# Loading the stacked queries of an attention half with one transfer instead of three

## The chip, the cores and the metric

The kernel runs on one core of a Trainium2 chip. The core has a matrix engine (TensorE, PE in the profile; its weight loads are listed apart as PEld), a vector engine (VectorE, DVE), a scalar engine (ScalarE, ACT), a general engine (GpSimd, POOL) and SyncE (SP), which in this kernel issues every transfer and does nothing else but pass on a few semaphores. Data lies in DRAM, in the on-chip memory SBUF (128 partitions) and in the eight accumulator banks of PSUM. Sixteen DMA engines move data between DRAM and SBUF.

The metric is the device time of one execution in microseconds, as the median of several runs. The kernel before takes 1583.15 us (three runs, 1582.33 to 1583.36).

## The reference

One input `x` of 2048 rows and 512 columns goes through an attention block with one shared key and value head and through a gated feed-forward block; a gate per row mixes the two.

```python
q = (x @ wq)            # 32 heads of 16 columns
k, v = x @ wk, x @ wv   # one head of 16 columns, shared by all 32
p = softmax(q @ k.T * 16 ** -0.5)
a = (p @ v, heads side by side) @ wo
b = (sigmoid(x @ w_gate) * (x @ w_up)) @ w_down      # 512 -> 1792 -> 512
g = sigmoid((x * gate_w).sum(-1))
out = g * a + (1 - g) * b
```

## The kernel before, in words

**Two numbers for one.** Products of projections and scores are made from a high part in the rounded type `fp32r` and a low part, the rest: `a*b` is taken as `hi*hi + hi*lo + lo*hi`. For the scores, whose inner dimension is a head's 16 columns, the three products are stacked into one inner dimension: three groups of 16 rows on each side, 48 rows in all. On the query side the stack is high part, high part again, low part. Rows 62 and 63 of each half of 64 partitions carry the high and low part of the negated row maximum.

**Units.** The 2048 queries are cut into 4 blocks of 512 (`TB`), and the 32 heads into 8 groups of 4 heads (`NG`). One block of one group is a unit; there are 32 (`NU`). A unit's four heads sit in two halves of the partitions (`par`, rows 0 to 47 and 64 to 111) with two heads beside each other in the free dimension (`pr`). A unit's stacked queries are the tile `qs`, 128 by 2 by 512; three such tiles take turns (`qs_t[u % 3]`).

**What happens to a unit's queries.** `query` multiplies a block with the query weights; `query_out` (lines 948 and 949) copies the result as the high part on ScalarE and takes the low part on VectorE. `store_q` (line 955) writes the two parts to a DRAM tile `qd`, which has room for two units. `load_q` (lines 969 and 971) fetches from it the rows of one unit into `qs`: for each half three transfers of 16 rows, the high part twice and the low part once, and from the fourth unit on a transfer that puts zeros into rows 62 and 63 (`qs` and `zeros`). Every row of such a transfer is 4 KB that lie together in DRAM. Then come the matmuls of `maximum` (line 1136), whose results VectorE reduces to row maxima (line 1138); the maxima go through GpSimd, VectorE and DRAM (`md`) and back into rows 62 and 63 (`place_max`, line 1002), and after that `scores` (line 1145) and the exponential on ScalarE (line 1147). Both kinds of matmul work on halves of the matrix engine: one on rows 0 to 63, one on rows 64 to 127, in turn.

**The order.** A planner in the kernel (class `State`) replays a string of codes, one code for a step of the matrix engine, and lays down the order of all instructions of all engines before anything is built; it carries due times of its own, and nothing is decided on the chip. Each engine runs its instructions in this order, and so does SP with its transfers. When a step of `load_q` comes is decided by the planner: as soon as the maxima of the unit before last are through (`load_next`), about one unit ahead of use except for the first two units, which are loaded right after the first two stores. The planner counts six issues and 384 KB for a unit; these numbers are not edited.

**SP's semaphores.** The transfers take eight semaphores in turn (`DMAHW0` to `DMAHW7`). A transfer that would take a semaphore waits until the transfer eight places before it has landed, and while it waits everything behind it on SP waits too. SP also relays between the two halves of a feed-forward bank: line 1114 is an empty instruction on SP that a matmul of the other half (line 1110) waits for.

**Two other loads have a form that matters here.** `vd<-od` (line 1039) and `bc<-rd` (line 1053) fetch 64 rows of 2 KB as four blocks of 16 rows: in DRAM the outermost count is 4, in SBUF it is 64 rows. All the other large transfers have the same number of rows, 16 or 128, outermost on both sides.

Of the kernel before, what the change touches and what calls it, by code (L numbers as in the profile page):

```python
# [9 lines left out]
F32 = mybir.dt.float32  # L10
# [7 lines left out]
S, D, H, DH, F = 2048, 512, 32, 16, 1792  # L18
P = 128
TB = 512  # L20
# [705 lines left out]
def tile_kernel(ctx, tc, x_in, wq, wkv, wo, wg, wu, wd, consts_in, out):  # L726
    nc = tc.nc

    def pool(name, bufs=1, **kw):
        return ctx.enter_context(tc.tile_pool(name=name, bufs=bufs, **kw))  # L730
# [5 lines left out]
    dp = pool("dp", space=DRAM)  # L736
# [137 lines left out]
    zeros = dp.tile([2, 2 * TB], F32, name="zeros")  # L874
# [11 lines left out]
    for o in (0, 64):  # L886
        nc.vector.tensor_copy(stack_of[:, :, o:o + 48].rearrange("p kc (i d) -> p kc i d", d=DH),
                              some[:, :, :DH].unsqueeze(2).to_broadcast([P, KC, 3, DH]))
        n = 8 if o else 9
# [51 lines left out]
    QD = {}  # L941
# [8 lines left out]

    def store_q(b, t):

        qd = dp.tile([2, 2, 2, DH, 2, TB], F32, name=f"qd{b}_{t}")
        for i, half in enumerate(QD[b, t]):
            nc.sync.dma_start(qd[i].rearrange("g par d pr t -> (g par d pr) t"), f32(half))
        QD[b, t] = qd

# [5 lines left out]
    def load_q(u):  # L963
        b, g = divmod(u, NG)
        qd, qs = QD[b, g // 2], f32(qs_t[u % 3]).rearrange("p pr t -> p (pr t)")
        for par in range(2):
            for n, i in enumerate((0, 0, 1)):
                r = 64 * par + n * DH
                nc.sync.dma_start(qs[r:r + DH], qd[i, g % 2, par].rearrange("d pr t -> d (pr t)"))
            if u > 2:  # L970
                nc.sync.dma_start(qs[64 * par + 62:64 * par + 64], zeros)
        MX[u] = ap.tile([P, 2, 2, NT, 4], F32, tag="mx", name=f"mx{u}", bufs=2)

    def max_finish(u):
# [165 lines left out]
    def scores(h, n, i):  # L1140
# [10 lines left out]
        "load_x": first_x, "x_first": first_hi, "xf": first_lo, "wq_first": wq_hi, "wq": wq_lo, "keys": on_bank(keys),  # L1151
        "query": on_bank(query), "turn": on_bank(turn), "keys_out": on_bank(keys_out), "query_out": on_bank(query_out),
        "turned": on_bank(turned), "store_q": store_q, "load_q": load_q, "add_sums": add_sums,
        "load": load_item, "w_hi": w_hi, "w": w_split, "x_hi": x_hi, "x": x_lo,
        "f": fill, "gate": gate, "gated": gated, "h": h_split, "part": part_of, "add": add_part, "out": send_out,
# [31 lines left out]
    for i in range(2):  # L1187
        for j in range(4):
            for t in (2 * i, 2 * i + 1):
                r, m = HALF[t % 2], slice(32 * j, 32 * j + 32)  # L1190
                nc.tensor.matmul(ps[t][m, :], o[i][r, m], WS["last"][r], start=True, stop=True)  # L1191
    BL = [BA.pop((NB - 1, t)) for t in range(NT)]
    for t in (1, 0, 2, 3):
        ba, g = BL[t], gsig[:, n0 + t:n0 + t + 1]
# [57 lines left out]
```

## Time and profile before

| | |
|---|---|
| time, median of three runs | 1583.15 us |
| time of the profiled execution | 1581.56 us |
| its span, first to last instruction | 1579.8 us |
| PE busy | 1570.6 us, 99% of the span |
| DVE busy | 1335.6 us, 85% |
| ACT busy | 1223.0 us, 77% |
| POOL busy | 785.7 us, 50% |
| DMA engines, mean busy share | about 21% |
| granted TensorE clock | 1.0 through the whole span |

The profile is one execution. Its span is 1.8 us shorter than the time of that execution and 3.4 us shorter than the median of the other runs. Times in it are microseconds from the first instruction unless marked ns. Rows of a timeline give start, duration, engine, line, operation and tiles (`out<-in`), then a count where like instructions are merged (`x12`, the duration then is that from the first start to the last end), and in brackets the idle time ahead of it and what ended that. SPq is SP's queue; a row of it is the issue of a transfer, not the transfer. Rows for a line give the shortest, median and longest duration in ns and the first and last start. PEldq is the queue of the matrix engine: an `EVENT_SEMAPHORE` there is a wait that stands in the program ahead of a matmul, because that matmul waits for more semaphores than one instruction can name.

### The profile page before, as it was taken

Reading aid. Unit: us, or ns where it says so; the run is one execution under the profiler, and the core shown is the slowest. Engines: PE = TensorE matmul, PEld = TensorE weight load, DVE = VectorE, ACT = ScalarE, POOL = GpSimd, SP = SyncE. Lnnn points to the kernel's source line nnn. Section 1 sums busy time; section 2 is a strip of 40 time slices with the busy share of each in tenths; the row PEclk is TensorE's granted clock in tenths of the full one; section 3 lists DMA queues with packets and bytes.
Section 4 is the critical chain, followed back from the end, with each engine's and each line's share of the span. In section 5 each row is a group of like instructions: output and inputs, shape, how many; then the busy total and the mean of one; then the engine's idle time right before and its main releaser. Section 6 shows DMA issues by size and latency. Waiting matters only on the chain.

```text
span 1579.8 us, 33611 instructions
## 1 busy us (share of the span) xinstructions
PE 1570.6 (99%) x12910; PEld 1018.7 (64%) x12910; DVE 1335.6 (85%) x2280; ACT 1223.0 (77%) x2415; POOL 785.7 (50%) x713
## 2 busy tenths in 40 slices
PE   9999999999999999999999999999999999999998
PEld 7776766666666665756665666666666667676663
DVE  7998998988798888889889878897978899898852
ACT  4276778878788778868788877877878888787897
POOL 4226463745574164367466236265657426537351
PEclk9999999999999999999999999999999999999999
DMA  7413120212122121122121212022212212111011
GB/s 254 154 55 91 45 62 30 66 53 89 42 80 61 48 80 52 33 73 73 47 82 53 76 36 85 16 66 67 75 42 89 66 34 79 53 36 56 16 56 48
DMA packets 63077, 103.44 MB, mean 65 GB/s; under 512 B 24530, under 2 KB 24786, under 8 KB 62916
## 3 DMA queue, kind: packets, MB, share of 16 engines
q1 hardware_dynamic: 62916, 101.29, 20.5%
q8 instruction: 102, 1.67, 0.4%
q14 instruction: 59, 0.48, 0.1%
HBM read 79.51 MB, written 21.75 MB: 64 GB/s over the span
## 4 chain that ended last, share of the span: by engine, by line
PE 98%; DVE 1%; DMA 0%; POOL 0%; issue 0%; ACT 0%; DVEq 0%; SPq 0%; ACTq 0%
PE bank L1110 32%; PE bank L1009 29%; PE bank L1136 17%; PE bank L1145 16%; PE bank L854 3%; DVE mx L1138 1%; PE bank L1191 0%; DMA wkv_raw<-wkv 0%; POOL wkv_s L757 0%; PE bank L926 0%; DVE q L949 0%; DVE wkv_stack L890 0%; DVE ba L1200 0%; DVEq L1248 0%; ACT ou_last L1173 0%
## 5 line engine op out<-in xcount | busy, mean ns | idle before, releaser
L1138 DVE TENSOR_REDUCE mx<-bank 128x1 f32<-128x512 f32 x2048 | 1249.7, 680 | 172.9 <-PE bank L1136 85.9
L1147 ACT ACTIVATE p<-bank 128x512 f32<-128x512 f32 x2048 | 1037.2, 661 | 4.5 <-PE bank L1145 1.4
L1145 PE MATMUL bank<-qs,ks 64*128 64x512 f32 x2048 | 721.6, 401 | 0.0
L1136 PE MATMUL bank<-ks,qs 64*128 64x512 f32 x2048 | 680.7, 407 | 0.0
L1009 PE MATMUL bank<-p,v_aug 128*32 128x512 f32 x4096 | 477.5, 597 | 0.0
L1136 PEld LDWEIGHTS bank<-ks,qs 64*128 64x128 f32 x2048 | 337.5, 184 | 133.2 <-issue 49.7
L1145 PEld LDWEIGHTS bank<-qs,ks 64*128 64x128 f32 x2048 | 358.7, 184 | 89.5 <-ACT p L1147 20.1
L1016 ACT COPY ou<-bank 128x512 f32<-128x512 f32 x194 | 117.0, 603 | 281.1 <-PE bank L1009 196.0
L1023 POOL TENSOR_TENSOR ou<-ou,ou 128x512 f32<-128x512 f32 x163 | 210.0, 1288 | 210.9 <-ACT ou L1016 207.8
L1110 PE MATMUL bank<-wd,hl 64*128 64x512 f32 x1344 | 278.3, 391 | 0.1
L1110 PE MATMUL bank<-x,wu 64*128 64x512 f32 x1344 | 278.0, 391 | 0.1
L1009 PEld LDWEIGHTS bank<-p,v_aug 128*32 128x32 f32 x4096 | 114.7, 109 | 253.5 <-issue 208.5
L1110 PE MATMUL bank<-x,wg 64*128 64x512 f32 x1344 | 275.2, 391 | 0.0
L1110 PEld LDWEIGHTS bank<-wd,hl 64*128 64x128 f32 x1344 | 204.0, 184 | 19.7 <-issue 4.2
L1110 PEld LDWEIGHTS bank<-x,wu 64*128 64x128 f32 x1344 | 203.5, 185 | 14.8 <-issue 1.7
L1110 PEld LDWEIGHTS bank<-x,wg 64*128 64x128 f32 x1344 | 201.8, 185 | 16.1 <-issue 2.0
L1089 POOL TENSOR_TENSOR ba<-ba,pa_d 128x512 f32<-128x512 f32 x31 | 39.6, 1284 | 102.8 <-ACT pa_d L1086 102.8
L830 POOL CAST wg<-rg 128x1024 fp32r<-128x1024 f32 x27 | 28.0, 1038 | 123.5 <-PE bank L1110 66.2
L757 POOL TENSOR_TENSOR wd<-rd,wd 128x512 fp32r<-128x512 f32 x56 | 72.3, 1291 | 4.5
L757 POOL TENSOR_TENSOR hl<-h,hl 128x512 fp32r<-128x512 f32 x56 | 71.9, 1284 | 4.5
L1110 PE MATMUL bank<-wa,o 64*128 64x512 f32 x360 | 71.4, 393 | 0.0
L830 POOL CAST wu<-ru 128x1024 fp32r<-128x1024 f32 x27 | 28.0, 1038 | 82.1 <-PE bank L1110 65.0
(82 smaller groups left out, 745.1 us busy)
## 6 DMA issues: line engine op xcount, KB each, us to landing
rg<-wg SPq DMA_DIRECT2D x28, 512.0 KB
ru<-wu SPq DMA_DIRECT2D x28, 512.0 KB
rd<-wd SPq DMA_DIRECT2D x28, 512.0 KB
qs<-qd SPq DMA_DIRECT2D x192, 64.0 KB
qd<-q SPq DMA_DIRECT2D x32, 256.0 KB
od<-ou SPq DMA_DIRECT2D x31, 256.0 KB
xf<-x_in SPq DMA_DIRECT2D x16, 256.0 KB
vd<-od SPq DMA_DIRECT2D x32, 128.0 KB
```

The costliest lines, as they stand in the source:

```text
L757: lo.tensor_tensor(hl[:, 1, :], raw, f32(hl[:, 0, :]), op=ALU.subtract)
L830: nc.gpsimd.tensor_copy(WS[item][:, 0, :], raw)
L854: nc.tensor.matmul(ps, w[:, p, part(kc)], X[b, kc][:, q, :], start=i == 0, stop=i == 3 * KC - 1)
L1009: nc.tensor.matmul(ps[32 * j:32 * j + 32, :], v_aug[:, c, :], PT.pop((u, c, j)), start=start, stop=stop)
L1016: nc.scalar.copy(to, ps)
L1023: nc.gpsimd.tensor_tensor(SUMS[u], SUMS[u], PARTS_OF[u].pop(0), op=ALU.add)
L1089: nc.gpsimd.tensor_tensor(BA[b, t], BA[b, t], PA[b, t].pop(0), op=ALU.add)
L1110: ins = nc.tensor.matmul(banks[i], l, r, start=start, stop=stop)
L1136: nc.tensor.matmul(banks[i], qs_t[u % 3][r, pr, part(qt)], ks[r, kb * 512:(kb + 1) * 512], start=True, stop=True)
L1138: nc.vector.tensor_reduce(MX[u][:, pr, h, qt, kb:kb + 1], banks[i], axis=AX.X, op=ALU.max)
L1145: nc.tensor.matmul(banks[i], ks[r, part(c)], qs_t[u % 3][r, pr, :], start=True, stop=True)
L1147: nc.scalar.activation(p, banks[i], AF.Exp, scale=0.25)
```

## The change

The DRAM tile `qd` gets a third part. `store_q` writes the high part twice and the low part once, so that the stack of three stands in DRAM in the order in which `qs` wants it. `load_q` then fetches the 48 rows of one half with a single transfer. The rows, their contents and their places in `qs` are the same, and so is the order of all other steps.

```diff
     def store_q(b, t):
 
-        qd = dp.tile([2, 2, 2, DH, 2, TB], F32, name=f"qd{b}_{t}")
-        for i, half in enumerate(QD[b, t]):
+        qd = dp.tile([3, 2, 2, DH, 2, TB], F32, name=f"qd{b}_{t}")
+        for i, half in enumerate((QD[b, t][0], *QD[b, t])):
             nc.sync.dma_start(qd[i].rearrange("g par d pr t -> (g par d pr) t"), f32(half))
         QD[b, t] = qd
...
         qd, qs = QD[b, g // 2], f32(qs_t[u % 3]).rearrange("p pr t -> p (pr t)")
         for par in range(2):
-            for n, i in enumerate((0, 0, 1)):
-                r = 64 * par + n * DH
-                nc.sync.dma_start(qs[r:r + DH], qd[i, g % 2, par].rearrange("d pr t -> d (pr t)"))
+            r = 64 * par
+            nc.sync.dma_start(qs[r:r + 3 * DH], qd[:, g % 2, par].rearrange("n d pr t -> n d (pr t)"))
             if u > 2:
-                nc.sync.dma_start(qs[64 * par + 62:64 * par + 64], zeros)
+                nc.sync.dma_start(qs[r + 62:r + 64], zeros)
```

The number of bytes loaded is unchanged, 384 KB for a unit in 2 transfers instead of 6. Each of the 16 stores (one for a block and two groups) becomes 3 transfers of 256 KB instead of 2, so 16 more transfers and 4 MB more written in all. The new load's outermost count is 3 in DRAM (three blocks of 16 rows of 4 KB, 256 KB apart) and 48 rows in SBUF.

SP's queue at the start, from the first stores to the transfers of the next block of `x`, before (`qd_0` and `qd_1` are the first two DRAM tiles, `qs_107` and `qs_108` the stacked queries of units 0 and 1, `xf` the raw `x`):

```order
L955 DMA qd_1_236<-q_1_1_221 128x512 [waits DMAHW1_49,DVE_49]
L969 DMA qs_107<-qd_0_204 16x1024 [waits DMAHW6_49,DMAHW2_49]
L969 DMA qs_107<-qd_0_204 16x1024 [waits DMAHW3_49]
L969 DMA qs_107<-qd_0_204 16x1024 [waits DMAHW7_49,DMAHW4_49]
L969 DMA qs_107<-qd_0_204 16x1024 [waits DMAHW5_49]
L969 DMA qs_107<-qd_0_204 16x1024 x2
L969 DMA qs_108<-qd_0_204 16x1024 [waits DMAHW0_49]
L969 DMA qs_108<-qd_0_204 16x1024 [waits DMAHW1_49]
```

The same place after the change, up to the fifth transfer of `xf`:

```order
L955 DMA qd_1_237<-q_1_1_222 128x512 [waits DMAHW3_49,DVE_49]
L968 DMA qs_107<-qd_0_204 48x1x1024 [waits DMAHW6_49,DMAHW7_49,DMAHW4_49,DMAHW0_49]
L968 DMA qs_107<-qd_0_204 48x1x1024 [waits DMAHW5_49]
L968 DMA qs_108<-qd_0_204 48x1x1024 x2
L955 DMA qd_2_263<-q_2_0_244 128x512 [waits Activation_49]
L955 DMA qd_2_263<-q_2_0_244 128x512 [waits DMAHW1_49]
L955 DMA qd_2_263<-q_2_1_245 128x512 [waits DMAHW2_49,DVE_49]
L766 DMA xf_0_267<-x_in 128x512 [waits DMAHW3_49]
L766 DMA xf_1_268<-x_in 128x512 [waits DMAHW4_49]
L766 DMA xf_2_269<-x_in 128x512 [waits DMAHW5_49]
L766 DMA xf_3_270<-x_in 128x512 [waits DMAHW6_49]
L766 DMA xf_0_275<-x_in 128x512 [waits DMAHW7_49]
```

Twelve loads have become four, which take the semaphores `DMAHW4` to `DMAHW7`; the third, fourth and fifth transfer of `xf` now wait for the landing of the second, third and fourth of them.

On the matrix engine, the first matmuls on unit 0's stacked queries, before (the first on rows 0 to 63, the second on rows 64 to 127, and so on in turn):

```order
L1136 MATMUL bank_79<-ks,qs_107 128x512 [waits DMAHW4_49,DMAHW3_49,DMAHW2_49]
L1136 MATMUL bank_72<-ks,qs_107 128x512 [waits DMAHW7_49,DMAHW6_49,DMAHW5_49]
L1136 MATMUL bank_73<-ks,qs_107 128x512
L1136 MATMUL bank_74<-ks,qs_107 128x512 [waits DVE_49]
```

and after:

```order
L1135 MATMUL bank_79<-ks,qs_107 128x512 [waits DMAHW4_49]
L1135 MATMUL bank_72<-ks,qs_107 128x512 [waits DMAHW5_49]
L1135 MATMUL bank_73<-ks,qs_107 128x512
L1135 MATMUL bank_74<-ks,qs_107 128x512 [waits DVE_49]
```

Each half's first matmul waits for one transfer instead of three; nothing has moved.

## Prediction

> **What bounds the kernel now.** I read the page first: its busy times and the chain that ended last, then whom the matrix engine waits for.
>
> ```profile
> span 1579.8 us, 33611 instructions
> ...
> PE 1570.6 (99%) x12910; PEld 1018.7 (64%) x12910; DVE 1335.6 (85%) x2280; ACT 1223.0 (77%) x2415; POOL 785.7 (50%) x713
> ...
> PE 98%; DVE 1%; DMA 0%; POOL 0%; issue 0%; ACT 0%; DVEq 0%; SPq 0%; ACTq 0%
> ```
>
> The matrix engine is busy for all but 1579.8 - 1570.6 = 9.2 us, and the chain runs along it from end to end. A transfer matters only where it makes this engine wait, and then each microsecond of waiting is one of time, since nothing later on the engine is idle to take it back. All its named waits are at the start and the end:
>
> ```profile
> PE bank L879 <- POOL v_aug L870: 1.3, 1, 1.3
> PE bank L854 <- POOL wkv_s L757: 0.8, 1, 0.8
> PE bank L1175 <- ACT ou_last L1173: 0.5, 1, 0.5
> PE bank L1184 <- DVE on L1182: 0.4, 1, 0.4
> ```
>
> No transfer is among them. But matmuls whose ends are modelled hide short waits, and the change touches the loads that the maxima of line 1136 wait for, so I looked at that line between 10 and 26 us, where unit 0 begins:
>
> ```profile
> L1136 PE MATMUL bank<-ks,qs x6: 383/430/498, 23.6 to 24.5; 64*128 64x512 f32 x6
> ...
> L1136 PEldq EVENT_SEMAPHORE  x2: 51/51/51, 23.1 to 23.8; - x2
> ```
>
> The second wait instruction ran at 23.8, after the first matmul had started at 23.6. By the order of the program it stands ahead of the first matmul on the lower half of the partitions and waits for that half's three loads. So at 23.8 the matrix engine is already released by unit 0's last load: there is no slack at this place. SP's queue ahead of it, with the work on VectorE that sets when the last store can go:
>
> ```profile
> 13.21 4.90 SPq L955 DMA_DIRECT2D qd<-q  x4
> 18.21 6.39 SPq L969 DMA_DIRECT2D qs<-qd  x12
> 24.70 0.84 SPq L955 DMA_DIRECT2D qd<-q  x2
> 25.59 3.81 SPq L766 DMA_DIRECT2D xf<-x_in  x8
> ...
> 17.09 0.68 DVE L949 TENSOR_TENSOR q<-bank,q 128x512 fp32r<-128x512 f32 x1
> ```
>
> Later units are loaded far ahead. The nearest is unit 12 (line 1136 between 562 and 579 us):
>
> ```profile
> 561.99 1.26 SPq L969 DMA_DIRECT2D qs<-qd  x3
> ...
> 563.61 1.23 SPq L969 DMA_DIRECT2D qs<-qd  x3
> ...
> L1136 PEldq EVENT_SEMAPHORE  x4: 51/51/51, 576.7 to 577.0; - x4
> ```
>
> Its loads begin at 562.0 and are first asked for at 576.7, 14.7 us later.
>
> **The change, part by part.**
>
> *Issues on SP.* A load's issue takes a median of 0.413 us; the form with blocks outermost, to which the new load belongs, takes 0.562.
>
> ```profile
> L969 SPq DMA_DIRECT2D qs<-qd x192: 303/413/1422, 18.2 to 1453.6; - x192
> L1053 SPq DMA_DIRECT2D bc<-rd x32: 507/562/575, 155.8 to 1552.6; - x32
> ```
>
> A unit's loads go from 6 x 0.413 = 2.48 us to 2 x 0.562 = 1.12 us, 1.36 us less of SP's time 32 times. That is worth what the matrix engine waits for SP, through the relay on line 1114:
>
> ```profile
> L1114 SPq EVENT_SEMAPHORE  x192: 17/17/17, 72.2 to 1555.1; - x192
> ...
>   PEld bank L1110: 1.2, 3
> ```
>
> Three waits of its weight loads, 1.2 us in all: between 0 and -1.2 us. I take 0, because 192 relays lie among 32 loads and only three are late. The wait instructions that leave the matrix engine's queue (one per half and unit, 51 ns) ran ahead of the matmuls while it was busy: 0.
>
> *The third store.* It adds an issue of about a third of a microsecond and 256 KB. At the start it goes while VectorE still makes the low part (17.09 + 0.68 = 17.77, after which the last store follows), so the loads still begin at 18.2: 0. Between 26 and 34 us the transfers are the limit of their own:
>
> ```profile
> 26.00:34.00 8.00, 8.00 (x38) 5.56 (x38) 7.64 (x14) 3.07 (x6) 1.30 (x2) 1.00 0.98 309
> ```
>
> The last two columns are the DMA engines' share and GB/s: 256 KB more is 0.85 us there. What is loaded in that stretch is used later, which covers it:
>
> ```profile
> 32.00 2.18 ACT L781 CAST x<-xf 128x512 fp32r<-128x512 f32 x4
> ...
> 32.70 10.04 POOL L787 TENSOR_TENSOR x<-xf,x 128x512 fp32r<-128x512 f32 x8 [17.88 <-ACT x L781]
> ...
> 40.45 2.60 PEld L854 LDWEIGHTS bank<-x,wkv_s 128*128 128x128 f32 x12
> ```
>
> GpSimd makes four low parts in half of 10.04 us, until 37.7; they are first used at 40.45. If transfers there slip by more than 2.7 us, this cover is gone.
>
> *The load itself.* This is the term that counts. Before, 16 rows per transfer land one by one. A load with blocks outermost is already there, `bc` with its four blocks of 16 rows, 128 KB in all:
>
> ```profile
> 581.31 0.56 SPq L1053 DMA_DIRECT2D bc<-rd  x1
> ...
> 585.11 1.29 POOL L1058 TENSOR_TENSOR vd<-vd,bc 128x512 f32<-128x512 f32 x1 [2.41 <-DMA bc<-rd]
> ...
> 1335.39 0.56 SPq L1053 DMA_DIRECT2D bc<-rd  x1
> ...
> 1340.06 1.29 POOL L1058 TENSOR_TENSOR vd<-vd,bc 128x512 f32<-128x512 f32 x1 [2.96 <-DMA bc<-rd]
> ```
>
> From issue to the waiting instruction 3.80 and 4.67 us. A store of 256 KB with 128 rows outermost takes 2.12 us until the transfer that waits for it is issued:
>
> ```profile
> 569.58 0.43 SPq L1032 DMA_DIRECT2D od<-ou  x1
> ...
> 571.70 0.57 SPq L1039 DMA_DIRECT2D vd<-od  x1
> ```
>
> Twice the bytes in half the time. The view of the DMA queues shows why, between 625.3 and 626.8 us and then in the middle of it, 625.7 to 626.3, while only a `bc` is under way:
>
> ```profile
> DMA packets 59, 0.12 MB, mean 78 GB/s; under 512 B 2, under 2 KB 2, under 8 KB 59
> ...
> q1 hardware_dynamic: 59, 0.12, 24.2%
> ```
>
> ```profile
> DMA packets 24, 0.05 MB, mean 82 GB/s; under 512 B 0, under 2 KB 0, under 8 KB 24
> ...
> q1 hardware_dynamic: 24, 0.05, 21.0%
> ```
>
> 24.2% of 16 engines is 3.9: a transfer of four blocks keeps four engines busy. In the second window 21.0% is 3.4 engines and 82 GB/s, 24.4 GB/s for each. From this I estimate that the new load, three blocks, runs on three engines: 192 KB / 3 = 64 KB for each, 65.5 / 24.4 = 2.69 us. The two halves' loads follow each other on the same three engines, 5.37 us together. What a `bc` takes beside its data is 3.80 - 32.8 / 24.4 = 2.46 us; what the 256 KB store takes is 2.12 - 16.4 / 24.4 = 1.45 us.
>
> [...] No run so far shows a transfer with 3.
>
> So the second half's load lands at 18.2 + 2.46 + 5.37 = 26.0, and the wait that ran at 23.8 runs at 26.0: **+2.2 us**. The ends: with the store's 1.45 us beside the data 25.0, +1.2 us; with the slower `bc` (4.67, so 3.33 beside the data) 26.9, +3.1 us; at the 309 / 16 = 19.3 GB/s per engine of the crowded window 3.39 us per load, 27.5, +3.7 us. I take 2.2, from the load that has the same form and a quiet queue. In every later unit the pair is through 2.46 + 5.37 = 7.8 us after its issue, inside the 14.7 us of unit 12: 0.
>
> *What waits behind it.* Unit 1's two loads go on the same three engines, until 28.7 and 31.4. By the order after, the transfers of `xf` that come third to fifth wait for those landings: the fifth goes at 31.4 instead of about 27.5, the fourth, the last that the matmuls at 40.45 need, at 28.7 instead of about 27.0. 1.7 us late against 2.7 us of cover, and the matrix engine itself is 2.2 us later: 0, but not by far.
>
> The sum is 0 + 0 + 2.2 + 0 = +2.2 us on the profiled execution's 1581.56, 1583.8. The median of the runs is 1.6 us above that execution, so 1583.15 + 2.2 = **1585.35**. A change of under 0.2%, 3.2 us, is about what a measurement of this kernel can't tell from none.
>
> **The rivals.**
>
> 1. *The transfer is spread over all the engines after all* (48 rows in SBUF allow it, 3 blocks in DRAM speak against it, as does `bc`). Then the second load, issued about 18.8, lands by 18.8 + 2.1 = 20.9, the wait at 23.8 goes, and the matrix engine gains the 0.2 us between 23.6 and 23.8: 1582.95. The change then does what it says and finds nothing to win. 9%.
> 2. *Slower by more: the stall grows or the cover at 40.45 breaks.* One mechanism, SP held behind slow loads at the start. It decides from the point where the fourth `xf` slips by more than 2.7 + 2.2 = 4.9 us, or at 19.3 GB/s, where the first stall alone is 3.7 us. With 3.39 us per load unit 1's first lands at 18.2 + 2.46 + 3 x 3.39 = 30.8, so the fourth `xf` is 3.8 us late, still inside; a microsecond more and the matmuls at 40.45 wait too. That gives +3.7 to +5.5 us, 1586.9 to 1588.7. For it: the DMA share of 0.98 right behind. Against: only three engines read in the stretch before. 20%.
> 3. *Faster: SP was the hidden brake.* The freed 1.36 us per unit would have to bring transfers and relays sooner for a matrix engine that waits for them. It decides at 3.2 us out of the 9.2 us that the engine isn't busy, of which the four waits above hold 3.0, and the relay 1.2 us. At its best -1.2 - 0.2 = -1.4 us from these rows, 1581.7; over 0.2% would need idle time that no row shows. 3%.
>
> **How the numbers follow.** The forecast, a single stall of 1.2 to 3.1 us at unit 0, has 68%: 1585.35, its own range 1584.35 to 1586.25. Rival 1 has 9%, rival 2 20%, rival 3 3%. Within 0.2% are the forecast and rival 1, 77%; slower by more is rival 2, 20%; faster rival 3, 3%. The range takes in rival 1 and the runs' own spread below it (0.3 us), 1582.6, and rival 2 up to its middle, 1587.8.
>
> **What would show it.** In the profile after, the second wait instruction of the first maxima stands near 26.0 instead of 23.8, with the first near 23.3, the matrix engine has a gap of some 2 us there, and everything behind is shifted by that much to the end. The four loads are issued in about 2.3 us from 18.2. A quiet stretch behind a later unit's loads shows about 3 of 16 engines busy, 19%, and line 1136 has half the wait instructions. The matmuls now at 40.45 start about 42.7 and not later. The prediction is wrong if the wait stands near 23.1 to 23.8 (rival 1), if it stands beyond 27 or the shift grows after it (rival 2), or if the shift is given back further on, which would mean that the matrix engine had hidden slack.

## The result, and the profile after

The changed kernel takes 1590.64 us, the median of five runs (1590.09 to 1595.11), against 1583.15 us of the kernel before beside it: a ratio of 1.0056, 95% interval 1.0045 to 1.0067. Timed a second time it took 1591.13 against 1581.75 us, 1.0057 (1.0044 to 1.0070). It is slower by 7.5 to 9.4 us, where 2.2 were forecast, and it lies above the range.

The page of the changed kernel, span, busy times and the chain that ended last:

```profile
span 1588.9 us, 33443 instructions
...
PE 1573.4 (99%) x12910; PEld 1019.5 (64%) x12910; DVE 1335.5 (84%) x2280; ACT 1223.7 (77%) x2415; POOL 785.7 (49%) x713
...
PE 95%; DMA 1%; DVE 1%; POOL 1%; ACT 0%; SPq 0%; issue 0%; DVEq 0%; ACTq 0%
```

The span grew by 9.1 us. Two things are to be seen. The matrix engine's idle time grew by 6.3 us (15.5 instead of 9.2), and its busy time by 2.8 us with the same 12910 matmuls: some of them ran slower. Whom it waits for:

```profile
PE bank L1135 <- DMA qs<-qd: 4.5, 2, 3.1
PE bank L879 <- POOL v_aug L870: 1.3, 1, 1.3
PE bank L1109 <- SPq L1113: 1.3, 2, 1.1
```

(Lines 1109, 1113, 1135 and 1144 are 1110, 1114, 1136 and 1145 of the kernel before; in the kernels of the experiments they stand a few lines further down.) A transfer, the new load, now heads the list, and the relay on SP has become a named wait. Three places carry the loss.

**Unit 0.** The matrix engine's timeline before,

```profile
23.56 1.30 PE L1136 MATMUL bank<-ks,qs 64*128 64x512 f32 x6
24.79 3.02 PE L854 MATMUL bank<-x,wq 128*128 128x512 f32 x12
27.74 0.73 PE L1136 MATMUL bank<-ks,qs 64*128 64x512 f32 x4
```

and after:

```profile
24.96 0.50 PE L1135 MATMUL bank<-ks,qs 64*128 64x512 f32 x1 [1.37 <-DMA qs<-qd]
28.57 1.64 PE L1135 MATMUL bank<-ks,qs 64*128 64x512 f32 x5 [3.11 <-DMA qs<-qd]
30.14 5.31 PE L854 MATMUL bank<-x,wq 128*128 128x512 f32 x12
35.39 0.73 PE L1135 MATMUL bank<-ks,qs 64*128 64x512 f32 x4
```

The first half's load holds the engine until 24.96, the second's until 28.57. The last row of both tables is the same four matmuls: 35.39 - 27.74 = 7.65 us late. Of that the 12 matmuls of line 854 alone account for 5.31 - 3.02 = 2.29 us. They waited for nothing; the clock was slower. The windows of the same stretch (busy time of PE, PEld, DVE, ACT and POOL, then the granted clock, the DMA share and GB/s):

```profile
24.90:25.50 0.60, 0.50 (x1) 0.18 (x1) 0.26 (x1) 0.31 (x1) 0.00 (x0) 1.00 0.91 311
28.50:30.20 1.70, 1.63 (x6) 0.89 (x6) 0.80 (x2) 0.00 (x0) 0.00 (x0) 0.50 0.39 149
30.10:33.00 2.90, 2.90 (x8) 2.28 (x8) 2.38 (x4) 0.00 (x0) 0.00 (x0) 0.50 0.45 126
33.00:35.40 2.40, 2.40 (x9) 1.53 (x7) 0.00 (x0) 0.00 (x0) 0.00 (x0) 0.56 0.42 158
35.40:39.00 3.60, 3.60 (x18) 2.46 (x17) 2.83 (x5) 0.59 (x1) 0.00 (x0) 1.00 0.97 321
```

After the second wait the matrix engine is granted half its clock, until about 35 us: 1.37 us of waiting left the clock at 1.00, a further 3.11 us with one matmul of 0.50 us between brought 0.50.

SP's queue at this place:

```profile
18.33 3.02 SPq L968 DMA_DIRECT2D qs<-qd  x4
21.39 1.43 SPq L955 DMA_DIRECT2D qd<-q  x3
22.86 13.24 SPq L766 DMA_DIRECT2D xf<-x_in  x8
```

The loads are issued when they were before (18.21), so the third store costs nothing here. The eight transfers of `xf` took 13.24 us of SP's queue instead of 3.81.

**Unit 12, 550 us later.** Of the span's 9.1 us, 9.1 - 7.65 = 1.4 are lost, on balance, behind unit 0, and the named waits on SP place most of them at unit 12. SP's and GpSimd's queues there, after:

```profile
569.70 0.71 SPq L968 DMA_DIRECT2D qs<-qd  x1
...
570.95 0.73 SPq L968 DMA_DIRECT2D qs<-qd  x1
...
572.21 0.44 SPq L749 DMA_DIRECT2D rd<-wd  x1
```

```profile
580.32 0.61 POOL L756 CAST wd<-rd 128x512 fp32r<-128x512 f32 x1 [3.73 <-DMA rd<-wd]
```

and before:

```profile
565.28 0.40 SPq L749 DMA_DIRECT2D rd<-wd  x1
...
569.34 0.61 POOL L756 CAST wd<-rd 128x512 fp32r<-128x512 f32 x1 [0.46 <-DMA rd<-wd]
```

The weights `rd` of the next feed-forward step are issued right behind unit 12's loads. From issue to their first use it was 4.06 us, and it is 8.11. GpSimd waits 3.73 us for them instead of 0.46, and everything that it does next is late: other weights, and the maxima's sums that SP has to send on. SP, which takes its steps in order, reaches its relay late, and the matrix engine waits:

```profile
594.08 0.50 PE L1109 MATMUL bank<-x,wu 64*128 64x512 f32 x1 [1.06 <-SPq L1113]
```

**Unit 2** is the same on a smaller scale. `md<-sq`, 16 KB, is issued behind unit 2's loads, and `qs<-md` waits for its landing. Before and after:

```profile
74.79 0.34 SPq L994 DMA_DIRECT2D md<-sq  x1
...
76.78 1.49 SPq L1002 DMA_DIRECT2D qs<-md  x2
```

```profile
82.47 0.33 SPq L993 DMA_DIRECT2D md<-sq  x1
...
86.01 1.43 SPq L1001 DMA_DIRECT2D qs<-md  x2
```

2.0 us have become 3.5. No wait for it is named in this profile, but the first matmul of line 1144 starts at 89.09 where it started at 81.14 before, 7.95 us late instead of 7.65; in another profile of the same kernel the wait is named (below).

### The profile page after: what moved, and what is told of

Its sections match the earlier page's. It is cut to its first block, busy times and chain, and to the rows that moved or that the text cites. A ratio compares the mean times of both kernels' runs of the same rounds, so it can differ in the third digit from the quotient of the medians.

```text
span 1588.9 us, 33443 instructions
## 1 busy us (share of the span) xinstructions
PE 1573.4 (99%) x12910; PEld 1019.5 (64%) x12910; DVE 1335.5 (84%) x2280; ACT 1223.7 (77%) x2415; POOL 785.7 (49%) x713
## 4 chain that ended last, share of the span: by engine, by line
PE 95%; DMA 1%; DVE 1%; POOL 1%; ACT 0%; SPq 0%; issue 0%; DVEq 0%; ACTq 0%
PE bank L1109 32%; PE bank L1008 29%; PE bank L1135 16%; PE bank L1144 16%; PE bank L854 2%; DVE mx L1137 1%; DMA qs<-qd 1%; DMA rd<-wd 1%; DMA wqr<-wq 0%; POOL wd L757 0%; POOL wu L831 0%; POOL wg L831 0%; DVE q L949 0%; ACT x L781 0%; PE bank L1190 0%
```

## The experiments

The theory that the profile after gives: the new load runs on three DMA engines and lands late. It costs a wait at unit 0, a halved clock behind that wait, and at units 2 and 12 it holds up other transfers that have a share on the same three engines. The rivals were the third store, SP, and "a single transfer of 48 rows is slow whatever its form". Times are medians of up to 11 runs; a ratio is to the kernel before on the same chip.

**The third store alone.** Three loads of 16 rows as before, the store kept.

```diff
-            nc.sync.dma_start(qs[r:r + 3 * DH], qd[:, g % 2, par].rearrange("n d pr t -> n d (pr t)"))
+            for n in range(3):
+                nc.sync.dma_start(qs[r + n * DH:r + n * DH + DH], qd[n, g % 2, par].rearrange("d pr t -> d (pr t)"))
```

> The third store is kept, the loads are three transfers of 16 rows as before, from the three parts. Theory (the store is covered): 1583.0 to 1583.8 us. Rival (16 more stores of 256 KB in the crowded start are the cost): 1586 or more.

Measured 1582.68 us, ratio 1.0001 (0.9992 to 1.0010); the kernel before took 1582.69 beside it, 0.5 us less than beside the changed kernel. The 16 more stores cost nothing that can be measured; the load is to blame.

**One load of the same bytes, 16 rows outermost.** The three copies of a row lie side by side in `qs`, so that the transfer has 16 outermost in DRAM instead of 3 (48 rows in SBUF as before), and the stack of the keys and the row of signs are put in the same order.

```diff
-            nc.sync.dma_start(qs[r:r + 3 * DH], qd[:, g % 2, par].rearrange("n d pr t -> n d (pr t)"))
+            nc.sync.dma_start(qs[r:r + 3 * DH], qd[:, g % 2, par].rearrange("n d pr t -> d n (pr t)"))
```

> The changed kernel with the 48 rows in another order: the head's column outermost and the three parts inside it, so that the one transfer has 16 outermost in DRAM instead of 3 (the stacked keys and their masks are ordered alike). Theory (three blocks put the load on three DMA engines): the load lands some 2.5 to 3 us after its issue, the wait instruction of the second half stands at or below 23.8, the stall and the half clock are gone: 1582.5 to 1583.8 us. Rival (a transfer of 48 rows is slow in whatever order, by its size or its form): stays at 1589 to 1591.

Measured 1581.69 us, ratio 0.9994 (0.9985 to 1.0003). The same two transfers, the same 192 KB each, the same third store, and the loss is gone. In its timeline the six first maxima run in one piece, with no wait for the load:

```profile
25.53 0.97 PE L1135 MATMUL bank<-ks,qs 64*128 64x512 f32 x6
```

What counts is not one transfer instead of three but the 3 in its outermost dimension in DRAM.

**Only units 0 and 1 by one load**, the others by three.

```diff
+            if u < 2:
                 nc.sync.dma_start(qs[r:r + 3 * DH], qd[:, g % 2, par].rearrange("n d pr t -> n d (pr t)"))
+            else:
+                for n in range(3):
+                    nc.sync.dma_start(qs[r + n * DH:r + n * DH + DH], qd[n, g % 2, par].rearrange("d pr t -> d (pr t)"))
```

> Third store kept; units 0 and 1 are loaded by one transfer per half, all later units by three. Theory: the whole cost of the start, 1583.2 + 7.6 = 1590.8, or a little less. Rival (cost spread over all the units): 1584 or less.

Measured 1588.93 us, ratio 1.0037 (1.0025 to 1.0050). It is less than expected and leaves something for the later units.

**Only the later units by one load**, units 0 and 1 by three (`if u > 1:` in the place of `if u < 2:`).

> Third store kept; units 0 and 1 are loaded by three transfers per half, all later units by one. Theory (the start costs 7.6 us, a transfer queued behind the slow loads of unit 12 costs 1.4 us): 1584.2 to 1585.0. Rival (the cost is spread over all the units): 1589 or more. Rival of the prediction (later units cost nothing): 1583.2.

Measured 1585.40 us, ratio 1.0020 (1.0011 to 1.0029), 0.4 us over the end of what was expected. The two halves add up: 0.37% + 0.20% = 0.57%, as the whole change. The profile of this kernel has the late weights again, 576.39 - 566.98 = 9.41 us after their issue, and the waits that follow on the matrix engine:

```profile
566.98 0.41 SPq L749 DMA_DIRECT2D rd<-wd  x1
```

```profile
576.39 0.61 POOL L756 CAST wd<-rd 128x512 fp32r<-128x512 f32 x1 [5.05 <-DMA rd<-wd]
```

```profile
585.05 0.50 PE L1148 MATMUL bank<-qs,ks 64*128 64x512 f32 x1 [1.58 <-DVE mx L1141]
...
589.92 0.50 PE L1113 MATMUL bank<-x,wu 64*128 64x512 f32 x1 [0.75 <-SPq L1117]
```

**The same, but unit 12 by three loads** (`if u > 1 and u != 12:`).

> As the kernel that changes from unit 2 on alone (1585.40 us), but unit 12 is loaded by three transfers again. Theory that the loss of the later units lies at unit 12, where the weight load issued right behind the two slow loads lands 3.3 us later and GpSimd, SP and the weights behind it are late: 1583.2 us (1582.6 to 1584.0). Rival, that the loss of the later units is spread over many of them, or made by the third store: 1585.4 (1584.9 to 1586.0).

Measured 1582.58 us, ratio 1.0005 (0.9996 to 1.0014). One unit out of thirty takes away 0.15%, about 2.4 us. Set against the kernel before matmul by matmul, the profiles give the step at this unit as 1.8 and 2.3 us in the two of the changed kernel and 2.9 in the kernel that changes from unit 2 on; with three loads in unit 12 there is none. GpSimd's wait for the same weights is short again, 571.31 - 567.17 = 4.14 us after their issue:

```profile
567.17 0.40 SPq L749 DMA_DIRECT2D rd<-wd  x1
```

```profile
571.31 0.61 POOL L756 CAST wd<-rd 128x512 fp32r<-128x512 f32 x1 [0.52 <-DMA rd<-wd]
```

**Units 2 and 12 by three loads as well as 0 and 1** (`if u > 1 and u not in (2, 12):`).

> One load per half from unit 3 on, but units 0, 1, 2 and 12 by three. Theory that transfers queued behind the slow loads cost at two places, the sums of the maxima stored behind unit 2's loads (0.7 us) and the weights loaded behind unit 12's (2 to 2.8 us): nothing is left of the steady cost, 1582.7 us or the kernel before within 0.5 us (the shift against before stays at the profile's level of before 80 us, without steps of more than 0.3 us at 80 or 582 us). Rival, that the 28 other units cost a little each: 1583.5 or more.

Measured 1582.24 us, ratio 0.9998 (0.9989 to 1.0007). The other 28 units take the slow load and cost nothing that can be measured. Unit 2's own part, 0.07% between this kernel and the one ahead of it, lies within the intervals; that it costs something is seen in the profiles. Matmul by matmul the step there is 0.2 and 0.6 us in the two of the changed kernel, 0.5 in the kernel that changes from unit 2 on, 0.7 in the one with unit 12 mended and none here. In the one with unit 12 mended the wait is named:

```profile
83.23 0.47 PE L1148 MATMUL bank<-qs,ks 64*128 64x512 f32 x1 [0.39 <-DMA qs<-md]
```

**The halved clock by itself.** In the changed kernel, 4 and 11 matmuls of the identity by itself are put ahead of unit 0's first maximum of either half, where the engine stands idle. Their results are overwritten; the waits for the loads stay.

```diff
         r = HALF[h]
+        for _ in range({0: 4, 1: 11}[h] if s == 0 and pr == 0 else 0):
+            nc.tensor.matmul(banks[i][:, :P], ident, ident, start=True, stop=True)
         nc.tensor.matmul(banks[i], qs_t[u % 3][r, pr, part(qt)], ks[r, kb * 512:(kb + 1) * 512],
```

> The kernel after, with matmuls of the identity by itself (4 of 128 columns ahead of unit 0's first maximum of the upper half, 11 ahead of that of the lower half) put into the two places where the matrix engine stands idle for 1.4 and 3.1 us. Nothing that is loaded, and no wait on a load, is changed: the second maximum still waits until 28.6 us. Theory that half of the granted clock between 25 and 32 us is a cost of its own (12 matmuls of line 854 took 5.31 us instead of 3.02, the 5 before them 1.6 instead of about 1.1): the granted clock stays 1.0 in these windows and the time is 1587.8 us, 2.8 less than the kernel after (1586.8 to 1588.8). Rival, the stall alone carries the loss and the clock's drop costs nothing behind it: 1590.6 (1590.0 to 1591.2). Either way the wait for the load stays.

> The kernel after again, beside the kernel with the filler matmuls, on the same chip: 1590.6 us (1589.5 to 1591.5). It is the mark that the filler's time is held against.

Measured 1590.41 us with filler (1589.11 to 1592.02) and 1591.13 without (1590.65 to 1591.70): 0.7 us where 2.8 were expected, with runs that overlap: the time lies in the range of the rival. The clock itself did what was expected, 1.00 throughout, and the 12 matmuls of line 854 took 3.01 us:

```profile
28.84 3.01 PE L854 MATMUL bank<-x,wq 128*128 128x512 f32 x12
31.79 0.73 PE L1137 MATMUL bank<-ks,qs 64*128 64x512 f32 x4
```

At 31.79 the engine is 2.9 us ahead of the kernel without filler timed beside it:

```profile
34.73 0.73 PE L1135 MATMUL bank<-ks,qs 64*128 64x512 f32 x4
```

But it then meets unit 2's late transfer, and the wait is 0.28 us without filler and 0.93 with it:

```profile
88.88 0.47 PE L1144 MATMUL bank<-qs,ks 64*128 64x512 f32 x1 [0.28 <-DMA qs<-md]
```

```profile
86.57 0.46 PE L1146 MATMUL bank<-qs,ks 64*128 64x512 f32 x1 [0.93 <-DMA qs<-md]
```

So part of the gain is taken back by the later waits, at unit 2 and again at unit 12. Of the 2.9 us, 1.7 are left in the two profiled spans (1587.3 and 1589.0 us). To see the clock's cost without these waits, the filler went into the kernel with only units 0 and 1 by one load.

> Units 0 and 1 by one load per half, all later units by three (so that no transfer of a later unit queues behind a slow load), and the 15 filler matmuls in unit 0's stall. Theory that the halved granted clock costs 2.9 us, which reach the end where no later wait takes them back: 2.9 us less than the same kernel without filler, 1586.0 us (1585.2 to 1587.0). Rival, that the 2.9 us are given back in any case: as without filler, 1588.9 (1588.0 to 1589.8).

> The kernel that changes in units 0 and 1 alone, again and without filler, on the same chip as the one with filler: 1588.9 us (1587.8 to 1589.7), 7 us over the kernel before in the profile.

With filler it took 1587.21 us, 0.2 over the end of what was expected, ratio 1.0025 (1.0015 to 1.0035); without, 1589.17 us and 1.0037 (1.0025 to 1.0050). The profiled execution of the first took 7043.82 us and can't be read, so the kernel ran again:

> Units 0 and 1 by one load per half and the 15 filler matmuls, again, for a profile in which unit 0's stall can be read. Theory: granted clock 1.0 from 24 to 36 us, the matrix engine's shift against the kernel before 4.0 us behind the stall instead of 6.9, and as little of it given back later as without filler, so about 1586.2 us (1585.0 to 1587.5). Rival, that waits further on take the 2.9 us back: the shift grows again by 2 us or more after 40 us and the time is 1588.5 or more.

Measured 1585.57 us, ratio 1.0024 (1.0015 to 1.0033), with the profiled span at 1583.5 us against 1586.8 without filler. The windows without filler and with it:

```profile
25.00:28.00 3.00, 0.48 (x1) 0.16 (x1) 0.89 (x2) 0.59 (x1) 0.00 (x0) 1.00 0.68 195
28.00:30.00 2.00, 1.44 (x5) 0.83 (x5) 0.61 (x2) 0.00 (x0) 0.00 (x0) 0.58 0.38 104
30.00:33.00 3.00, 3.00 (x8) 2.31 (x8) 2.47 (x5) 0.00 (x0) 0.00 (x0) 0.50 0.48 157
33.00:36.00 3.00, 3.00 (x11) 1.83 (x9) 0.00 (x0) 0.45 (x1) 0.00 (x0) 0.64 0.48 155
```

```profile
28.00:30.00 2.00, 1.82 (x9) 1.28 (x10) 1.29 (x3) 0.00 (x0) 0.00 (x0) 1.00 0.42 160
30.00:33.00 3.00, 3.00 (x15) 1.97 (x14) 1.99 (x4) 0.59 (x1) 0.00 (x0) 1.00 0.44 153
33.00:36.00 3.00, 3.00 (x16) 2.20 (x16) 2.88 (x5) 0.20 (x1) 0.00 (x0) 1.00 0.51 175
```

Useless matmuls in a wait make the kernel faster by 0.0013 of 1582 us, 2.1 us, by the ratios and by 3.3 us by the spans: the halved clock costs 2 to 3 us here. The intervals of the two ratios overlap, so the size rests on the profiles too: the four matmuls that stood at 27.74 before stand at 35.39 without filler and at 32.02 with it, and no later wait takes the difference back. What stays with filler, 0.24% or 3.8 us, is the wait proper.

**The high part read twice by one transfer.** From the kernel before: no third store; one transfer reads each of the 16 high rows twice, into 32 rows with the copies side by side, and one reads the low part. The keys' stack and the signs follow.

```diff
-            for n, i in enumerate((0, 0, 1)):
-                r = 64 * par + n * DH
-                nc.sync.dma_start(qs[r:r + DH], qd[i, g % 2, par].rearrange("d pr t -> d (pr t)"))
+            r = 64 * par
+            high, low = (qd[i, g % 2, par].rearrange("d pr t -> d (pr t)") for i in range(2))
+            nc.sync.dma_start(qs[r:r + 2 * DH], high.unsqueeze(1).to_broadcast([DH, 2, 2 * TB]))
+            nc.sync.dma_start(qs[r + 2 * DH:r + 3 * DH], low)
```

> From the kernel before: the high part is stored once, and its 16 rows are loaded twice by one transfer that reads each row twice (32 rows, order changed so that a row's two copies lie side by side, the slowest dimension 16), the low part by one of 16 rows: two issues per half instead of three, no third store. Theory that only the slowest dimension of a transfer counts: no stall, granted clock 1.0 throughout, and less time on SP: 1582.2 us (1581.5 to 1583.0). Rival, that 32 rows by one transfer are slow however their dimensions stand: a stall of at least 2 us at unit 0, 1585 or more.

Measured 1582.92 us, ratio 1.0004 (0.9995 to 1.0013). The rival is out. Fewer issues on SP bring nothing either, and neither this kernel nor the one with 16 rows outermost can be told from the kernel before: no version here is faster than it.

## Why the prediction was wrong

**What bounds the kernel: right.** The matrix engine is the chain, and most of the waiting put into it came out at the end. That there is no slack at unit 0 holds too: in the profile of the kernel with unit 12 mended the first maxima wait 0.73 us even for the three old loads.

**SP's issues, the wait instructions, the third store, all at 0: right.** The store alone gave 1.0001, and two kernels with fewer issues 0.9994 and 1.0004. The new load's issue takes 0.73 us, not the 0.562 of `bc`, so a unit saves 1.0 and not 1.36 us of SP; it hangs on nothing.

**Three DMA engines: right.** A quiet stretch behind unit 2's loads, after:

```profile
79.50:82.40 2.90, 2.90 (x14) 2.39 (x13) 2.87 (x7) 0.19 (x1) 0.42 (x2) 1.00 0.19 64
```

The DMA share is 0.19, 3 of 16 engines, as forecast. No run ahead of the prediction had three blocks: the three engines were an estimate from the 3.9 that `bc` with its four blocks kept busy. For the kernel with 16 rows outermost only its time, 1581.69 us, and the missing wait are shown, not the number of engines.

**The term that was mis-sized: "So the second half's load lands at 18.2 + 2.46 + 5.37 = 26.0 ... +2.2 us".** The matmul behind it started at 28.57. From the issue at 18.33 to the first half's matmul were 6.6 us, not 2.46 + 2.69 = 5.15, and 3.61 us more to the second's, not 2.69. With 64 KB for each of three engines that is 18 GB/s, below the 24.4 read from `bc` and close to the 19.3 of the prediction's crowded window, from which the upper end of 3.7 us came. Against 23.8 the wait is 4.8 us late, and 3.7 was given as the end. The crowd at this place isn't needed for it. Behind unit 28's two loads, between 1316.7 and 1324 us of the changed kernel, hardly anything but their 393 KB moves:

```profile
DMA packets 104, 0.40 MB, mean 54 GB/s; under 512 B 7, under 2 KB 7, under 8 KB 104
```

54 GB/s are 18 for each of three engines, and the pair takes some 7.2 us, 3.6 for a load, as at unit 0; the quiet window behind unit 2's loads gives 64 / 3 = 21. So the number that failed is the 24.4 GB/s for each engine, read from 0.6 us of a `bc` and carried over to another form; why the new load moves less for each engine stays open. If the first load ran at the second's rate, the time beside the data was 6.6 - 3.6 = 3.0 us, not 2.46.

**The term that was missing: the clock.** The sum had no line for what a wait of 3 us does to the matmuls behind it. It was worth 2 to 3 us, about as much as the whole forecast. The rivals had none either.

**The step that fell: "In every later unit the pair is through ... 7.8 us after its issue, inside the 14.7 us of unit 12: 0".** The maxima of unit 12 indeed never waited for their load. The question was put to the wrong reader: the load's own user has slack, but the transfer queued behind it has not. Unit 12 costs 0.15%, and unit 2 a little.

**"What waits behind it": right, but by luck.** `xf` was late on SP by much more than forecast (its last issue ends at 36.1 instead of 29.4), yet the weight loads that stood at 40.45 run without a wait, because the matrix engine itself was 7.65 us late:

```profile
48.10 2.60 PEld L854 LDWEIGHTS bank<-x,wkv_s 128*128 128x128 f32 x12
```

48.10 - 40.45 is 7.65 again.

**The rivals.** That the transfer is spread and that SP was the brake are both out. Rival 2 had the sign and "the stall grows", but not the mechanism: the cover at 40.45 held, and its 1586.9 to 1588.7 us were too low. What the prediction named as its own refutation, a wait beyond 27 and a shift that grows after it, is what the profile shows.

The whole, by the experiments: 3.8 us of wait at unit 0, 2 to 3 us of halved clock, about 2.4 us at unit 12 and up to 1.1 at unit 2 (0.07%), 8 to 10 us beside the 7.5 to 9.4 measured. The changed kernel's own profile has 7.65 us at unit 0, wait and clock together, 0.2 at unit 2 and 1.8 at unit 12, and some 0.5 us are given back by the end.

## What to carry to other kernels

Before merging transfers, look at the outermost dimension in DRAM: with 16 there one transfer of 192 KB was as good as three of 64 KB (ratio 0.9994), with 3 the same bytes ran on 3 of 16 engines (DMA share 0.19). Take the rate for each engine from a transfer of the same form, or call it unknown. Ask of a slow transfer not only who waits for it but which transfers are issued behind it and how much slack their users have. And when a change makes the matrix engine wait for some 3 us, price the halved clock behind it too, here 2 to 3 us; matmuls of nothing in the wait are a way to measure it.

## What the runs showed of the hardware

**Transfers queue behind a narrow one.** `rd<-wd`, 512 KB, took 4.06 us from issue to use behind loads of 16 rows and 8.11 and 9.41 us behind the narrow ones. The trace of the changed kernel shows how far the wide transfer gets beside them. `rd` is 256 rows of 2 KB, and the loads are rows of 4 KB. From 573.29 to 576.00 us 208 packets of 2 KB start, 13 sixteenths of `rd`, and then none until 577.72, while the 4 KB packets of unit 12's loads go on until 578.33:

```profile
576.00:577.00 1.00, 1.00 (x12) 0.81 (x10) 1.00 (x3) 1.00 (x4) 0.59 (x1) 1.00 0.19 72
577.00:578.00 1.00, 1.00 (x11) 0.66 (x10) 1.00 (x3) 1.00 (x4) 0.00 (x0) 1.00 0.20 76
```

With a share of 0.19 to 0.20, 3 of 16 engines are at work, and GpSimd waits until 580.32 for the rest of `rd`, 48 rows, 3 sixteenths. That these rows stand in line on the three engines of the loads is the author's reading: the numbers of the engines aren't in the trace.

**The clock moves in steps of 3.41 us.** In the traces' records of the granted clock every stretch between two changes is a whole number of steps of 3.41 us: 23.89, 6.83 and 1553.06 us in the changed kernel, 7, 2 and 455 steps, and 1573.54 us before, 461. In all four profiles with the long wait at unit 0 (two of the changed kernel, two with units 0 and 1 alone) the half clock lasts 6.83 us, two steps: from 28.29 to 35.12 in the first. The step before this fall, from 24.87 on, had the matrix engine busy for 0.50 us, and in the second profile of the changed kernel for 1.25; a step with 2.13 us, from 21.46 to 24.87, left the clock alone. In the first step at half the engine was busy for 3.13 us, in the second profile for 1.00, and both times the clock came back only behind a second step that was busy throughout. In these two profiles the fall stands at 28.29 and about 26.5, 0.3 and 2.4 us ahead of the matmul that ended the wait, and the 12 matmuls of line 854 behind it took 5.31 and 4.33 us: how a wait lies against these steps differs between executions of one kernel, and with it what the half clock costs.

**A second start.** Two of the profiled executions are 2 us late before any changed instruction, those of the kernel that changes from unit 2 on and of the one with 16 rows outermost. The nine matmuls of line 854 in the first 12 us took 2.33 us before and 3.69 in the former:

```profile
7.21 2.33 PE L854 MATMUL bank<-x,wkv_s 128*128 128x512 f32 x9
```

```profile
7.90 3.69 PE L854 MATMUL bank<-x,wkv_s 128*128 128x512 f32 x9
```

In these two the traces' first record of a granted clock of 1.0 stands at 10.86 and 10.65 us, in the other profiles between 4.35 and 6.93 (before: 5.33); a 1.00 in a window ahead of that means only that there is no record. Between 7.9 and 10.8 us a matmul of line 854 took 628 ns in the median, against 395 in the kernel before, and from 8 to 10 us the windows count 7 matmuls in either of the two against 10 before. So the clock comes later in some executions. This is part of the 2 to 3 us by which runs of one kernel differ, and a reason to compare medians and not two spans; why it comes later stays open.
